# One batch's load in two transfers, weight blocks split beside two chunks, and some stages and closing sums at other places in the order

## The chip, the cores and the metric

The kernel runs on one core of one Trainium2 chip. The metric is the device time of one execution in microseconds, as the median of several executions. The engines of the core are named as in the profile: PE is TensorE (matmul; PEld its weight loads), DVE is VectorE, ACT is ScalarE, POOL is GpSimd, SP is SyncE, whose queue (SPq) issues most DMAs.

## The reference

```python
batch, seq, dim = (8, 3008, 256)          # x, float32
n_tokens, d_model, d_ff = (24064, 256, 2048)

X = np.fft.fft(x, axis=1)
X = np.fft.fft(X, axis=2)
attn = X.real.astype(np.float32)          # then reshaped to (24064, 256)

h = x @ w_in
relu6 = np.clip(h + 3.0, 0.0, 6.0)
g = h * relu6 / 6.0
return (g @ w_out).astype(np.float32)
```

So: a real part of a two-dimensional Fourier transform of each batch (over 3008 rows and 256 columns), and on its rows a two-layer MLP with a hardswish between the layers, all in float32.

## The kernel before

**Work and tiles.** The eight batches are taken as four pairs. The transform over 3008 = 47 x 64 rows has two stages. Stage 1 (`stage1`, eight blocks `c` per pair) works on four of the 64 columns at a time: SP loads x forward (`load_forward`, two transfers for the two batches of the pair, into partitions 0 to 63 and 64 on), POOL gathers the mirrored rows (`load_partners`), POOL adds and subtracts the two (`fold`, tiles `xt` and `y`), PE multiplies by a 47-row table, ACT and DVE copy the two PSUM banks to `z`, and SP sends `z` to a scratch in DRAM (`zd`). Stage 2 (`stage2`) loads it back turned round (`load_g`) and multiplies by 64-row tables; `split_q` writes its result as three parts into `KQ` (ACT the high part, DVE in `split_rest` the two others). The transform over the 256 columns is folded into `w_in`.

A pair has 12 chunks of about 256 rows (the chunk's number over all pairs is `n_all`, 0 to 47), a chunk eight steps `fc`, one for each 256 of the 2048 hidden columns. The first layer runs in units: PE adds the three passes of `KQ` times `KW` into the bank `u` (first the even half, then the odd one), ACT has put a first value into it (`seed`, u<-QN), a copy `s` of the even half is kept (`keep_even`), DVE forms the other sign `v` from `s` and `u` (`other_sign`), ACT takes the two ReLUs `t`, and DVE writes the gated hidden values into `A` (`gates`). The second layer multiplies 2 x 2 blocks with seven products (`mlp2`), of which POOL forms the sums `c` (`combine`). From chunk 8 on the first two of the seven products are not taken as float32 matmuls but as three passes each of a split operand `J` (`split_gates`: ACT twice, DVE twice) with split weights `GH` and `GK` (`split_weights`, once for each `fc`: ACT and DVE on 128 x 256 values, with a scratch bank `high`). At a chunk's end the seven sums are joined (`close`, parts 0 to 4: e<-acc, freeing the accumulator banks `acc` for the next chunk), POOL adds (`finish`), DVE transposes and SP sends the result (`store`).

**Order.** Every engine's order is written out by hand. From step `SPLIT` on the main loop runs in cycles, one unit each, with seven products of the second layer spread over it (six in the chunks before number 8); a cycle takes the pieces of the surrounding stages at fixed places: `products(1)`, `other_sign`, `close_to`, `passes`, `gates`, `products(size - 4)`, then the matmuls of stage 1 (`next(gen)`), `products(2)`, `split_rest`, `seed` of the unit after next, and the rest of stage 1. When the blocks of a pair are loaded and folded is decided by `Feed` and `fold_pieces`, which hold a planned backlog of POOL below a limit; `beside` puts stage 2 of chunk n at the step `when[n]`, counted from the unit that first uses it. The folding of pair p+1 lies in the chunks of pair p, on POOL between the sums `c`.

Of the kernel before, what the change touches and what calls it, by code (L numbers as in the profile page):

```python
# [60 lines left out]
def kernel(  # L61
# [121 lines left out]
    def load_forward(pr, c):  # L183
        xt = x_tile(xpool, "xf", 1)
        n = XC if c < NXC - 1 else XC - 1
        for b in range(2):

            i = 2 * pr.p + b
            nr = N1 + 1 if i < B - 1 else N1

            if b == 0:
                nr = PB
            rows, o = x_pn[i * N1:i * N1 + nr], xt[b * PB:b * PB + nr]
            nc.sync.dma_start(out=o[:, 0:n, :], in_=rows[:, c * XC + 1:c * XC + 1 + n, :])
            if n < XC:
                nc.sync.dma_start(out=o[:, n:XC, :], in_=rows[:, 0:1, :])
        pr.x[c] = xt
# [112 lines left out]
    def stage1(pr, c):  # L310
        y = pr.y[c]
        ps = [bank([P, 2, D], "ps1"), other_bank([P, 2, D], "ps1")]
        for h in range(2):
            last = (c, h) == (NXC - 1, 1)
            for b in range(2):
                n = 1 if last else 2
                nc.tensor.matmul(ps[b][h * PB:(h + 1) * PB, 0:n], table(0, b), y[rows(b), 2 * h:2 * h + n],  # L317
                                 start=True, stop=not last, skip_group_check=last)


            cosine, sine = slice(0, P + 1), slice(P + 1, D)
            for k, (j, cs) in enumerate([(XC - 1, cosine), (XC, cosine), (XC - 1, sine), (XC, sine)] if last else ()):
                for b in range(2):
                    nc.tensor.matmul(ps[b][h * PB:(h + 1) * PB, 1, cs], table(k + 1, b), y[rows(b), j, cs],
                                     start=False, stop=(k % 2 == 1), skip_group_check=True)
        z = zpool.tile([PB + PZ, 2, 2, D], F32, tag="z", name="z")
        nc.scalar.copy(z[:, 1], ps[1][0:PB + PZ])
# [233 lines left out]
    class Chunk:  # L561
# [3 lines left out]
        def __init__(self, pr, ck):  # L565
# [8 lines left out]
            self.n_all = pr.p * NCK + ck  # L574
            self.split, self.gated = self.n_all >= CHUNK2, {}
            k1 = [(ck * KK + j // 2 + 1) % NK1 for j in range(KC)]
# [234 lines left out]
    HIGH, OTHERS = (0,), (2, 1)  # L811

    def order_of(ch, fc):

        end = ch.final and fc == NF - 1
        if not ch.split:
            return [[(i, None)] for i in range(7)]
# [56 lines left out]
    def split_weights(fc):  # L874
# [9 lines left out]
        yield  # L884
        nc.scalar.mul(rest, ps[:], 1.0 / (1.0 + EPS))

    closing, freed = [], []

    def close_to(end):
        while closing and closing[0][1] < end:  # L890
            close(*closing[0])
            closing[0][1] += 1
            if closing[0][1] == 5:
                closing.pop()

    def close(ch, part):
# [12 lines left out]
        elif part == 3:  # L909
            plus(e[:, 5], 5, e[:, 0], -1.0)  # L910
        else:
            plus(e[:, 4], 4, e[:, 5])
            plus(e[:, 6], 6, e[:, 5])
            ch.r = {(m, h): ch.e[:, (1, 6, 2, 3)[2 * m + h]] for m in range(2) for h in range(2)}
# [332 lines left out]
    def beside():  # L1247
# [26 lines left out]
        for n in range(NSG, NP * NCK):  # L1274
# [9 lines left out]
            if i == 0:  # L1284
                put(max(t - 7, before + 1), load_t, gr)
                put(max(t - (6 if gr else 5), before + 1), load_g, pr, gr)
            put(t, stage2, pr, gr, i, at=middle_fns)
# [196 lines left out]
    for un in units:  # L1484
        for ch, _ in un.parts:
            first_use.setdefault(ch.n_all, place[max(un.i - 1, 0)] // 7)
    when = {n: first_use[n] - 7 for n in first_use}
    when[NSG - 1], when[NSG], when[NSG + 1] = 17, 23, 27
    prev = None
# [26 lines left out]
    for s in range(SPLIT):  # L1516
# [11 lines left out]
        else:  # L1528
# [7 lines left out]
            if prev and not prev.first:  # L1536
                turns_out(s)
            elif prev and 3 <= fc < 7:
                store(prev, (fc - 3) // 2, 1 - fc % 2)
            mlp2(*chunk(s), 0, 3)  # L1540
# [5 lines left out]
            mlp2(*chunk(s), 3, 7)  # L1546
            close_to(5)
        if fc == NF - 1:
# [5 lines left out]

    gates_of = {s: split_gates(*chunk(s)) for s in range(CHUNK2 * NF, len(steps))}
    high_of, others_of, others_at, start = [], [], 0, 0
    seed(units[1])
    weights_of = list(range(NF))

# [22 lines left out]
    def products(n):  # L1582
        nonlocal done, others_at
        for s, i in stream[done:done + n]:
# [4 lines left out]
            if fc == 0 and i == 6:  # L1589
                close_to(5)  # L1590
            flush(high_of, s)
# [4 lines left out]
            if i == 0:  # L1596
                high_of.extend(after.get(s, ()))
            if i in last or not last and i == 6:
                others_of.extend(after.get(s, ()))
# [4 lines left out]
    while done < len(stream):  # L1604
# [15 lines left out]
        flush(high_of)  # L1620
        if un:
            other_sign(un)
        close_to(5)
        if others_at > 4:
# [33 lines left out]
        split_rest()  # L1658
        if cycle + 2 < len(units):
            seed(units[cycle + 2])  # L1660
# [116 lines left out]
```

## Time and profile before

| | |
|---|---|
| median of three runs | 1820.53 us (1820.37 to 1821.40) |
| the profiled execution | 1819.84 us |
| its span, first to last instruction | 1818.1 us |
| mean granted TensorE clock | 0.997 |
| busy: PE, PEld, DVE, ACT, POOL | 98%, 84%, 81%, 76%, 72% |

Some 1.7 us of the profiled execution lie around the span. Idle time of PE is what can be saved; idle time of another engine counts only where PE waits for it. In the profile a row of the waits names who waited, for whom, the total, how often, and the longest; a row of the timeline has the start, the length, the engine, the line and the tiles, and in brackets the idle time before it and what ended it. Line numbers are those of the kernel before.

### The profile page before, as it was taken

The page shows a single profiled execution, that of the slowest core. Times are in us where ns is not written, and L with a number is a line of the kernel's source. Part 1 is how long each engine was busy: PE and PEld are TensorE (multiplying, and loading weights), DVE is VectorE, ACT ScalarE, POOL GpSimd, SP SyncE. Part 2 cuts the span into 40 slices and gives each one's busy share as a digit, 9 for nine tenths or more (in the row PEclk, how much of TensorE's full clock was granted, in tenths as well). Part 3 has the DMA queues.
Part 4 walks back from the last instruction along what each step waited for, and adds up shares of the span by engine and source line. Part 5 has one row for each costly group of instructions (what it writes and reads, how often), then busy time and mean ns, then how long its engine had stood idle before and what let it go on. Part 6 is the DMA issues. An engine that isn't in the chain of part 4 may idle for free.

```text
span 1818.1 us, 29912 instructions
## 1 busy us (share of the span) xinstructions
PE 1783.8 (98%) x9664; PEld 1524.8 (84%) x9664; DVE 1472.0 (81%) x2789; ACT 1382.1 (76%) x2496; POOL 1305.3 (72%) x1468
## 2 busy tenths in 40 slices
PE   9999999999999999999999999999999999999997
PEld 6678888868898888888898777888889888888897
DVE  8978555688888888888888777878888888888887
ACT  6556666678888788788888777778888888888884
POOL 5686787777678889766767877876766666676674
PEclk9999999999999999999999999999999999999999
DMA  8433341321213233111012232311101101101001
GB/s 276 117 95 80 94 107 46 75 58 47 47 38 90 68 80 86 46 44 44 15 48 79 65 76 56 81 43 47 38 21 48 36 21 44 42 18 45 20 14 32
DMA packets 160538, 110.36 MB, mean 61 GB/s; under 512 B 122292, under 2 KB 141074, under 8 KB 160382
## 3 DMA queue, kind: packets, MB, share of 16 engines
q1 hardware_dynamic: 151630, 82.22, 18.0%
q0 software_dynamic: 7504, 25.65, 4.6%
q8 instruction: 76, 1.25, 0.3%
q10 hardware_dynamic: 1248, 0.59, 0.1%
q14 instruction: 80, 0.66, 0.1%
HBM read 71.93 MB, written 36.79 MB: 60 GB/s over the span
## 4 chain that ended last, share of the span: by engine, by line
PE 85%; DVE 5%; DMA 3%; ACT 2%; POOL 2%; issue 1%; SPq 1%; ACTq 0%; DVEq 0%; POOLq 0%
PE acc L841 52%; PE u L702 24%; DMA xt<-in_x_dram 2%; PE ps L551 2%; PE ps L317 2%; PE acc L802 1%; POOL c L792 1%; PE v L601 1%; ACT t L775 1%; PE u L601 1%; DVE v L735 1%; SPq L963 1%; PE spare L1081 0%; DVE J L868 0%; DVE J L869 0%
## 5 line engine op out<-in xcount | busy, mean ns | idle before, releaser
L841 PE MATMUL acc<-c,G 128*128 128x256 f32 (+1 forms) x3008 | 766.5, 377 | 15.3 <-POOL c L792 11.3
L702 PE MATMUL u<-KQ,KW 128*128 128x512 f32 (+6 forms) x2448 | 744.7, 419 | 2.6 <-ACT s L725 2.6
L792 POOL TENSOR_TENSOR c<-A 128x512 f32<-128x512 f32 (+1 forms) x357 | 451.2, 1264 | 329.7 <-PE acc L841 309.5
L841 PEld LDWEIGHTS acc<-c,G 128*128 128x128 f32 x3008 | 535.4, 190 | 101.4 <-POOL c L792 22.2
L702 PEld LDWEIGHTS u<-KQ,KW 128*128 128x128 f32 (+1 forms) x2448 | 432.5, 189 | 67.1 <-ACT s L725 5.0
L775 ACT ACTIVATE t<-u,half 128x512 f32<-128x512 f32 (+2 forms) x384 | 260.8, 679 | 198.7 <-PE u L702 135.1
L735 DVE SCALAR_TENSOR_TENSOR v<-s,u 128x512 f32<-128x512 f32 (+1 forms) x360 | 246.9, 686 | 176.3 <-ACT t L775 172.4
L775 ACT ACTIVATE t<-v,half 128x512 f32<-128x512 f32 (+2 forms) x384 | 261.6, 681 | 134.0 <-DVE v L735 133.1
L778 DVE SCALAR_TENSOR_TENSOR A<-t,v 128x512 f32<-128x512 f32 (+3 forms) x478 | 250.1, 544 | 40.4 <-ACT t L775 38.5
L792 POOL TENSOR_TENSOR c<-c,A 128x256 f32<-128x256 f32 (+1 forms) x357 | 258.6, 724 | 28.0
L792 POOL TENSOR_TENSOR c<-A,c 128x256 f32<-128x256 f32 (+1 forms) x357 | 258.0, 723 | 28.0
L868 DVE SCALAR_TENSOR_TENSOR J<-high,A 128x512 fp32r<-128x512 f32 (+1 forms) x315 | 212.3, 674 | 67.5 <-ACT high L867 39.8
L841 PE MATMUL acc<-J,GK 128*128 128x256 f32 (+1 forms) x1260 | 257.7, 327 | 1.9 <-DVE J L869 1.7
L778 DVE SCALAR_TENSOR_TENSOR A<-t,u 128x512 f32<-128x512 f32 (+3 forms) x478 | 248.2, 540 | 0.0
L717 ACT ACTIVATE u<-QN,WN 128x512 f32<-128x512 f32 (+1 forms) x312 | 216.8, 695 | 0.3
L841 PE MATMUL acc<-A,G 128*128 128x256 f32 (+1 forms) x720 | 211.7, 375 | 0.5 <-DVE e L901 0.5
L869 DVE SCALAR_TENSOR_TENSOR J<-high,A 128x512 fp32r<-128x512 f32 (+1 forms) x315 | 210.7, 669 | 0.0
L841 PEld LDWEIGHTS acc<-J,GK 128*128 128x128 f32 x1260 | 193.6, 190 | 18.8 <-DVE J L869 3.8
L862 ACT ACTIVATE J<-A 128x512 fp32r<-128x512 f32 (+1 forms) x315 | 193.2, 613 | 0.0
L867 ACT COPY high<-J 128x512 f32<-128x512 f32 (+1 forms) x315 | 186.0, 590 | 8.8 <-DVE KQ L869 5.7
L725 ACT COPY s<-u 128x512 f32<-128x512 f32 (+2 forms) x315 | 179.2, 569 | 0.0
L841 PEld LDWEIGHTS acc<-J,GH 128*128 128x128 f32 x630 | 117.2, 189 | 25.0
(176 smaller groups left out, 1750.0 us busy)
## 6 DMA issues: line engine op xcount, KB each, us to landing
out_dram<-o SPq DMA_DIRECT2D x744, 32.0 KB
T<-in_c_stage_dram SPq DMA_DIRECT2D x26, 512.0 KB
g<-zd SPq DMA_DIRECT2D x42, 256.0 KB
zd<-z SPq DMA_DIRECT2D x48, 192.0 KB
QN<-qd SPq DMA_DIRECT2D x43, 128.0 KB
xt<-in_x_dram SPq DMA_DIRECT2D x21, 256.0 KB
st<-in_moe_w_out_dram POOLq DMA_DIRECT2D x7, 512.0 KB, 6.2
xt<-in_x_dram SPq DMA_DIRECT2D x17, 192.0 KB
```

The lines of the kernel that those rows point to most:

```text
L702: nc.tensor.matmul(un.wide(un.u[:]) if un.joint else un.u[:, i, 0:un.nq], un.weights(j, blk, i, rows), un.moving(j, blk, rows), start=Fals ...
L717: nc.scalar.activation(un.wide(un.u[:]), un.wide(row), AF.Identity, scale=WN[:, f:f + 1])
L725: copy(un.wide(un.s[:]), un.wide(un.u[:]))
L735: nc.vector.scalar_tensor_tensor(v, s, -2.0, u, op0=AL.mult, op1=AL.add)
L775: nc.scalar.activation(t, h, AF.Relu, bias=half[:], scale=scale)
L778: nc.vector.scalar_tensor_tensor(dst, t, 1.0, h, op0=AL.min, op1=AL.mult)
L792: (eng or nc.gpsimd).tensor_tensor(out, in0, in1, op=AL.add)
L841: nc.tensor.matmul(o, w, moving[i] if j is None else parts_tile(ch, fc)[:, j, i, 0:ch.n], start=(fc == 0 and i % 2 == 0 and j in (None, 0) ...
L862: nc.scalar.mul(high, a, 1.0 - EPS / 2.0)
L867: nc.scalar.copy(ps, high.bitcast(F32))
L868: nc.vector.scalar_tensor_tensor(low, ps, -1.0, a, op0=AL.mult, op1=AL.add)
L869: nc.vector.scalar_tensor_tensor(rest, ps, 1.0 + EPS, a, op0=AL.mult, op1=AL.subtract)
```

## The change

Seven edits, all in the order of things or in the engine that does them:

- **Load.** Where a batch's transfer has not more than 47 rows (only the last batch of the last pair: the others have 48 or 64), it is cut into one of 32 rows and one of 15.
- **Which products are split.** An even `fc` takes the split form from chunk 8 on as before, an odd one from chunk 9 on; the weights of the even ones are split beside chunk 7, those of the odd ones beside chunk 8, and none in a cycle in which a chunk ends.
- **Last step of a weight's split** (`rest`): DVE in place of ACT.
- **Closing sums.** The last part of `close` is cut in two: the sum of product 4 comes ahead of `other_sign`, that of product 6 behind it.
- **First chunk of a later pair.** Its stage 2 comes one step earlier (the load for it stays where it was).
- **Stage 1.** Its matmuls stand one product later where the step before had a stage 2; its copies come one further point later, behind the seed of the unit after next.
- **Store of the first chunk**: the transposes of its second half one step later.

```diff
 # load_forward
-            nc.sync.dma_start(out=o[:, 0:n, :], in_=rows[:, c * XC + 1:c * XC + 1 + n, :])
-            if n < XC:
-                nc.sync.dma_start(out=o[:, n:XC, :], in_=rows[:, 0:1, :])
+            cut = nr if nr > N1 else N1 // 16 * 16
+            for r in (slice(0, cut), slice(cut, nr))[:1 + (cut < nr)]:
+                nc.sync.dma_start(out=o[r, 0:n, :], in_=rows[r, c * XC + 1:c * XC + 1 + n, :])
+                if n < XC:
+                    nc.sync.dma_start(out=o[r, n:XC, :], in_=rows[r, 0:1, :])
 # stage1, between the matmuls and the copies
+        yield
         z = zpool.tile([PB + PZ, 2, 2, D], F32, tag="z", name="z")
 # order_of, the planner and the main loop
+    def split_of(ch, fc):
+        return ch.n_all >= CHUNK2 + fc % 2
-        if not ch.split:
+        if not split_of(ch, fc):
...
-    weights_of = list(range(NF))
+    weights_of = [fc + (CHUNK2 - 1 + fc % 2) * NF for fc in (*range(0, NF, 2), *range(1, NF, 2))]
 # split_weights
-        nc.scalar.mul(rest, ps[:], 1.0 / (1.0 + EPS))
+        nc.vector.tensor_scalar(rest, ps[:], 1.0 / (1.0 + EPS), None, op0=AL.mult)
 # close
-        else:
-            plus(e[:, 4], 4, e[:, 5])
+        elif part == 4:
+            plus(e[:, 4], 4, e[:, 5])
+        else:
             plus(e[:, 6], 6, e[:, 5])
 # beside, and the steps of stage 2
-                put(max(t - (6 if gr else 5), before + 1), load_g, pr, gr)
+                put(max(t - (6 if gr else 4), before + 1), load_g, pr, gr)
+    for p in range(1, NP):
+        when[p * NCK] -= 1
 # the first chunk's store
-            elif prev and 3 <= fc < 7:
-                store(prev, (fc - 3) // 2, 1 - fc % 2)
+            elif prev and fc in (3, 4, 6, 7):
+                store(prev, fc // 5, (fc + 1) % 2 if fc < 5 else fc % 2)
 # the main loop's cycle
         if un:
+            close_to(5)
             other_sign(un)
-        close_to(5)
+        close_to(6)
...
-        if weights_of and not stages and done >= 7 * ((CHUNK2 - 1) * NF + weights_of[0] + 1 - SPLIT):
-            splitting = split_weights(weights_of.pop(0))
+        if weights_of and not stages and not ends and done >= 7 * (weights_of[0] + 1 - SPLIT):
+            splitting = split_weights(weights_of.pop(0) % NF)
...
-        products(size - 4)
+        behind_it = 1 if any(s - 1 in middle_fns for s in begun) else 2
+        products(size - 2 - behind_it)
         for gen in parts:
             next(gen)
-        products(2)
+        products(behind_it)
+        if parts and cycle + 2 < len(units):
+            seed(units[cycle + 2])
+        for gen in parts:
+            next(gen)
```

**Place 1, SP's queue** in the chunks of the third pair (where the last batch is loaded): `xt<-in_x_dram` are the forward loads, `out_dram<-o` the stores, `g<-zd` and `g<-zq` the loads of stage 2, `zd<-z` the sends of stage 1. Before:

```order
L963 DMA out_dram<-o 4x32x64 x6
L194 DMA xt<-in_x_dram 64x1024
L194 DMA xt<-in_x_dram 47x1024
L468 DMA g<-zd 64x4x256
L471 DMA g<-zq 64x4x1
L468 DMA g<-zd 64x4x256
```

and with the change:

```order
L971 DMA out_dram<-o 4x32x64 x6
L196 DMA xt<-in_x_dram 64x1024
L196 DMA xt<-in_x_dram 32x1024
L196 DMA xt<-in_x_dram 15x1024
L471 DMA g<-zd 64x4x256
L474 DMA g<-zq 64x4x1
L471 DMA g<-zd 64x4x256
```

The 47-row transfer has become one of 32 and one of 15 rows; the loads of stage 2 behind it stand one issue later, and nothing else in the queue has moved.

**Place 2, DVE** at the start of the second pair's first chunk: `J` are the two DVE steps of a product's split, `KQ` those of stage 2's result, `e<-acc` the closing sums of the chunk before. Before:

```order
L901 SCALAR_TENSOR_TENSOR e<-acc,e 128x256 x2
L868 SCALAR_TENSOR_TENSOR J<-high,A 128x512
L869 SCALAR_TENSOR_TENSOR J<-high,A 128x512
L639 SCALAR_TENSOR_TENSOR KQ<-ps_4376,KQ 128x2x256
L640 SCALAR_TENSOR_TENSOR KQ<-KQ,ps_4376 128x2x256
L735 SCALAR_TENSOR_TENSOR v<-s,u 128x450
L901 SCALAR_TENSOR_TENSOR e<-acc,e 128x256 x2
L778 SCALAR_TENSOR_TENSOR A<-t,u 128x256
```

and with the change:

```order
L908 SCALAR_TENSOR_TENSOR e<-acc,e 128x256 x2
L875 SCALAR_TENSOR_TENSOR J<-high,A 128x512
L876 SCALAR_TENSOR_TENSOR J<-high,A 128x512
L908 SCALAR_TENSOR_TENSOR e<-acc,e 128x256
L738 SCALAR_TENSOR_TENSOR v<-s,u 128x450
L908 SCALAR_TENSOR_TENSOR e<-acc,e 128x256
L781 SCALAR_TENSOR_TENSOR A<-t,u 128x256
```

The two KQ steps have left for the cycle before, and the two last closing sums stand on the two sides of `v`; at the other chunk ends only the second of these moves is found.

**Place 3, ACT** in chunk 7, where weights are split: `GK<-GH` and `GK<-high` are the first and last step of a weight's split, `u<-QN` the seed, `t` the ReLUs. Before:

```order
L725 COPY s<-u 128x512
L878 ACTIVATE GK<-GH 128x256
L717 ACTIVATE u<-QN,WN 128x512
L885 ACTIVATE GK<-high 128x256
L775 ACTIVATE t<-u,half 128x512
```

and with the change:

```order
L728 COPY s<-u 128x512
L885 ACTIVATE GK<-GH 128x256
L720 ACTIVATE u<-QN,WN 128x512
L778 ACTIVATE t<-u,half 128x512
L778 ACTIVATE t<-v,half 128x512
```

The last step of the split is gone from between the seed and the ReLU on ACT; on DVE it now stands behind the four steps that it depends on.

More of the change, by code (lines that the diff above doesn't have):

```diff
@@ L574, in __init__ @@
             self.n_all = pr.p * NCK + ck
-            self.split, self.gated = self.n_all >= CHUNK2, {}
+            self.gated = {}
             k1 = [(ck * KK + j // 2 + 1) % NK1 for j in range(KC)]
@@ L892, in close_to @@
             closing[0][1] += 1
-            if closing[0][1] == 5:
+            if closing[0][1] == 6:
                 closing.pop()
@@ L1553 @@
     done = 0
-    gates_of = {s: split_gates(*chunk(s)) for s in range(CHUNK2 * NF, len(steps))}
+    gates_of = {s: split_gates(*chunk(s)) for s in range(CHUNK2 * NF, len(steps)) if split_of(*chunk(s))}
     high_of, others_of, others_at, start = [], [], 0, 0
     seed(units[1])
-    weights_of = list(range(NF))
+    weights_of = [fc + (CHUNK2 - 1 + fc % 2) * NF for fc in (*range(0, NF, 2), *range(1, NF, 2))]
     def turn_before(s):
@@ L1589, in products @@
             if fc == 0 and i == 6:
-                close_to(5)
+                close_to(6)
             flush(high_of, s)
@@ L1597, in products @@
                 high_of.extend(after.get(s, ()))
-            if i in last or not last and i == 6:
+            if i in last or not last and i == 3:
                 others_of.extend(after.get(s, ()))
@@ L1621 @@
         if un:
+            close_to(5)
             other_sign(un)
-        close_to(5)
+        close_to(6)
         if others_at > 4:
@@ L1658 @@
         split_rest()
-        if cycle + 2 < len(units):
+        if not parts and cycle + 2 < len(units):
             seed(units[cycle + 2])
```

## The prediction

> **What bounds the kernel now.** I read the page's busy times first, then whom PE waited for, then equal stretches of the run against each other.
>
> ```profile
> PE 1783.8 (98%) x9664; PEld 1524.8 (84%) x9664; DVE 1472.0 (81%) x2789; ACT 1382.1 (76%) x2496; POOL 1305.3 (72%) x1468
> PE acc L841 <- POOL c L792: 11.3, 6, 3.8
> PE acc L841 <- DVE e L901: 3.3, 5, 0.9
> PE u L702 <- ACT s L725: 2.6, 5, 0.9
> PE v L601 <- DVE a L778: 2.5, 3, 2.0
> PE acc L841 <- DVE J L869: 1.7, 4, 0.7
> ```
>
> PE is busy for 1783.8 of 1818.1 us, so an order of things can win at most 34 us; the named waits hold 21 us of them, and half of that is one wait for POOL's sums c. The next view, busy time by stretch, says where. The stretches run from the start of chunk 12 to that of chunk 24 (pair 1), and from there to that of chunk 36 (pair 2): the same matmuls, 2327 in both.
>
> ```profile
> 461.20:893.30 432.10, 430.84 (x2327) 372.29 (x2325) 362.63 (x681) 351.66 (x634) 329.46 (x365) 1.00 0.23 58
> 893.30:1341.60 448.30, 435.63 (x2327) 373.79 (x2325) 363.42 (x681) 351.90 (x634) 328.62 (x365) 0.99 0.22 56
> ```
>
> Pair 2 takes 448.30 - 432.10 = 16.2 us more for equal work. What differs is the batch it loads beside: the last one, whose transfer has 47 rows where pair 1's has 48. In the waits from 993 to 1205 us, in those from 560 to 773 us, and in the chain of waits, the load is seen (rows in this order):
>
> ```profile
> POOL xt L271 <- DMA xt<-in_x_dram: 40.0, 7, 9.4
> POOL xt L271 <- DMA xt<-in_x_dram: 7.4, 4, 2.3
> 993.00 11.43 DMA xt<-in_x_dram
> ```
>
> POOL stands 40.0 us for x against 7.4 us, and one 47-row transfer takes 11.43 us. The timeline shows the same block of both pairs: SP issues the two loads, POOL then folds.
>
> ```profile
> 560.24 1.16 SPq L194 DMA_DIRECT2D xt<-in_x_dram  x2
> 565.10 1.27 POOL L271 TENSOR_TENSOR xt<-xt 111x508 f32<-111x508 f32 x1 [1.33 <-DMA xt<-in_x_dram]
> 992.41 1.02 SPq L194 DMA_DIRECT2D xt<-in_x_dram  x2
> 1004.59 1.26 POOL L271 TENSOR_TENSOR xt<-xt 111x508 f32<-111x508 f32 x1 [8.66 <-DMA xt<-in_x_dram]
> ```
>
> Pair 1 folds 565.10 - 560.24 = 4.9 us after the first issue, pair 2 only 12.2 us after it. During the landing, the stretches show (the last two columns are the share of the 16 DMA engines and GB/s)
>
> ```profile
> 561.60:563.80 2.20, 2.20 (x14) 1.94 (x14) 2.20 (x6) 1.96 (x4) 2.02 (x3) 1.00 0.87 224
> 999.60:1003.40 3.80, 3.80 (x22) 2.33 (x21) 1.74 (x4) 2.18 (x5) 0.00 (x0) 1.00 0.10 26
> 1007.70:1011.10 3.40, 2.92 (x9) 2.57 (x10) 0.76 (x2) 0.09 (x1) 3.24 (x5) 0.50 0.00 0
> 1130.60:1134.00 3.40, 3.40 (x10) 2.94 (x11) 1.26 (x2) 0.00 (x0) 3.32 (x5) 0.51 0.00 0
> ```
>
> 224 GB/s over nearly all engines in pair 1, and 26 GB/s over a tenth of them in pair 2, about what one or two engines of sixteen give. The sums c queue on POOL behind the fold, PE runs dry for up to 3.8 us, and after that its granted clock is 0.50 for 3.4 us, which costs another 1.7 us; the last row is the second such place.
>
> **The change part by part** (a minus is a gain).
>
> *The load, -16.0.* In the changed queue the last piece is issued one DMA later (half of 1.16 us, 0.6). If its 15 rows go the slow way, they take 15/47 of 11.43 = 3.6 us at most; if they spread as the 48 rows do, they land as in pair 1. So the fold comes between 4.9 + 0.6 = 5.5 and about 6.5 us after the first issue, not 12.2. PE's longest wait here was 3.8 us, so a fold up to 12.2 - 3.8 = 8.4 us after the issue stops nothing. Both ends clear it by 1.9 us or more, so I take all of the 16.2 but 0.2 for the extra issues on SP, which has idle time. Bounds: 14 to 16.2. Late next is nothing that pair 1 doesn't show, with 1.3 us of waiting at the fold and none of it on PE.
>
> The page "DMA: Bandwidth & Descriptors" of the Trainium skill (Why a DMA increments its semaphore by 16 and not by 1) says that a transfer runs on the largest number of engines up to 16 that divides its outermost size: 1 for 47, 16 for 48 and 32, 15 for 15. The 0.10 against 0.87 agrees; by it the 15 rows land early, and the sum would be 0.2 lower.
>
> *First chunk of pairs 1 to 3, -2.6.* DVE and PE there:
>
> ```profile
> 892.84 0.68 DVE L640 SCALAR_TENSOR_TENSOR KQ<-KQ,ps 128x512 fp32r<-128x512 f32 x1
> 893.43 0.62 DVE L735 SCALAR_TENSOR_TENSOR v<-s,u 128x450 f32<-128x450 f32 x1
> 893.97 0.75 DVE L901 SCALAR_TENSOR_TENSOR e<-acc,e 128x256 f32<-128x256 f32 x2
> 894.44 1.56 PE L841 MATMUL acc<-c,G 128*128 128x256 f32 x6 [0.86 <-DVE e L901]
> ```
>
> The closing sum frees the bank that PE wants 0.86 us earlier. With both KQ steps gone and one sum ahead of v, it is 2 x 0.6 + 0.5 = 1.7 us earlier, and the wait goes, at three places. The KQ steps fall into the cycle before, where DVE copies s early and v has a whole cycle of room. Bounds: -2.6 to -1.
>
> *A closing sum ahead of v, +1.2.* Everywhere else it pushes v, and behind it t<-v and s on ACT, by half of 0.75, which PE's next passes wait for. Two chunk ends show the room:
>
> ```profile
> 824.18 0.58 ACT L725 COPY s<-u 128x512 f32<-128x512 f32 x1
> 825.32 1.06 PE L702 MATMUL u<-KQ,KW 127*128 127x512 f32 x3
> 496.70 0.58 ACT L725 COPY s<-u 128x512 f32<-128x512 f32 x1
> 497.41 0.77 PE L702 MATMUL u<-KQ,KW 127*128 127x512 f32 x2
> ```
>
> The first has 825.32 - 824.76 = 0.56 us, enough for 0.37. The second, behind a pair's last chunk, has 0.13 and loses 0.25; that is found three times (0.75), and I add 0.45 for ends between the two. Bounds: 0.5 to 4.
>
> *Weights beside two chunks, -1.8.* The waits of PE from 340 to 420 us, where the weights are split and the split products begin:
>
> ```profile
> PE u L702 <- ACT s L725: 1.4, 2, 0.9
> PE acc L841 <- DVE J L869: 1.3, 3, 0.7
> PE acc L841 <- DVE e L901: 0.7, 2, 0.5
> 352.96 0.38 ACT L885 ACTIVATE GK<-high 128x256 fp32r<-128x256 f32 x1 [1.38 <-DVE high L883]
> ```
>
> Together 3.4 us. ACT's ReLU stands behind a step that waits 1.38 us for DVE; on DVE that step costs its own 0.4 us ahead of v instead. With a split in every other cycle and none at a chunk's end, I let 2.4 of the 3.4 go; the rest stays, since one cycle still has four or five weight steps, two J steps, v and the gates on DVE. Against it stand four odd fc of chunk 8 with float32 products. The chain of waits prices them (4 matmuls: 2 split and 2 float32; 12: 4 and 8):
>
> ```profile
> 557.19 0.67 PE acc L841 x4
> 558.56 2.20 PE acc L841 x12
> ```
>
> From 2s + 2f = 0.67 and 4s + 8f = 2.20, f = 0.215 and s = 0.12 us. Two products cost 4f = 0.86 in float32 and 6s = 0.72 split, so +0.14 for each fc, +0.6 in all. Bounds: -2.8 to +1.
>
> *Stage 1 and the store, 0.* ACT waits 1.47 us for stage 1's matmuls, and the seed (0.69) now stands in that gap:
>
> ```profile
> 594.14 0.59 ACT L327 COPY z<-ps 112x512 f32<-112x512 f32 x1 [1.47 <-PE ps L317]
> 595.40 0.69 ACT L717 ACTIVATE u<-QN,WN 128x512 f32<-128x512 f32 x1
> ```
>
> Without that cover, 0.69 us on ACT in 24 cycles. The 2.0 us for `a` at v L601 lie behind a weight step that stays. Bounds: -0.5 to +3.
>
> Sum: -16.0 - 2.6 + 1.2 - 1.8 = -19.2. From the profiled execution's 1819.84 us (span 1818.1) this gives 1800.6; the median of the runs lies 0.7 above it, so 1801.3.
>
> **The rivals.**
>
> *Slower: the time is one for each odd transfer, not for its rows* (0.05). Then the 15-row piece also takes 11.4 us, begins 0.6 us later, and decides as soon as it lands after what the 47 rows did. Eight folds later by 0.6 to 1.1 us (7 us, since PE is already dry there), and two more waits long enough to halve the clock (2 x 1.7), make +10.4; less 3.2 for the other edits, 1828. Against it: 26 GB/s in the landing says that bytes go through few engines.
>
> *The transfers are no faster cut in two* (0.07). All of the 16.2 stays, and the other edits give 1820.5 - 3.2 = 1817.3. The same page of the Trainium skill (Rules for kernel authors) says not to bother with two transfers to disjoint partitions, as both spray over the same 16 engines and serialize. This rule speaks against the change. For it in the trace: the pieces have one queue. Against it: the 47 rows are not spread at all, with 0.10 of the engines busy.
>
> *New waits take part of it* (0.07): the closing sum and the stage-1 copies both at their upper bounds, +2.8 and +3, the weights at +1 (2.8 worse) and the load at -14 (2 worse) give 1811.9.
>
> **How the numbers follow.** The main case has 0.81. Its lower end is every term at its good end: -16.2 - 2.6 + 0.5 - 2.8 - 0.5 = -21.6, 1798.9, less 2.4 if the waits for `a` and the last of the weights' go as well: 1796.5. Its upper end is 1809: load at -14 and two of the other terms bad. That holds 8 in 10. The measurement can tell 0.2%, 3.6 us, from no change: the main case and the third rival lie below 1816.9 (0.88), the second rival within (0.07), the first above (0.05).
>
> **What would show it.** Pair 2's twelve chunks at 432 to 434 us instead of 448.3; POOL's wait for x from 993 to 1205 us near 8 instead of 40 us; a granted clock of 1.00 all through; no wait for e at the starts of chunks 12, 24 and 36; under 1.5 us of PE's waits from 340 to 420. The prediction is wrong if the 15-row transfer lands later than 8 us after the first issue, or if PE waits for s or J at chunk ends or in stage-1 cycles by over 4 us in all.

## The result, and the profile after

| | before | after |
|---|---|---|
| median of the runs | 1820.76 us (1820.37 to 1821.40, 4 runs) | 1791.70 us (1791.60 to 1792.14, 4 runs) |
| the profiled execution, its span | 1819.84 us, 1818.1 us | 1791.71 us, 1789.9 us |
| mean granted TensorE clock | 0.997 | 0.999 |

The ratio is 0.9841, with a 95% interval of 0.9823 to 0.9858. The change gains 29.1 us, where 19.2 were forecast: the direction and the largest term are right, and the time lies 4.8 us below the lower end of the range.

The page's busy times after, then of e_load (the load edit alone, see below), and four rows of PE's waits in the whole run after (those left out lie in the first 26 us or come to 0.2 us):

```profile
PE 1773.1 (99%) x9656; PEld 1519.5 (85%) x9656; DVE 1468.3 (82%) x2789; ACT 1374.6 (77%) x2480; POOL 1306.4 (73%) x1468
PE 1778.8 (99%) x9664; PEld 1523.9 (85%) x9664; DVE 1470.5 (82%) x2789; ACT 1381.5 (77%) x2496; POOL 1306.5 (72%) x1468
PE acc L848 <- DVE c L795: 2.0, 2, 1.0
PE u L705 <- ACT s L728: 1.2, 3, 0.4
PE acc L848 <- DVE J L876: 0.6, 2, 0.4
PE v L604 <- DVE a L781: 0.5, 2, 0.3
```

PE's 11.3 us of waiting for POOL's c have gone, and so has all waiting for e. But PE's busy time fell too, from 1783.8 to 1773.1 us, with 8 matmuls fewer of 9664. So the 1783.8 were not all work. The load edit alone takes 5.0 of these 10.7 us, nearly all in the third pair, whose mean granted clock was 0.99 before and is 1.00 with the load cut. The other edits take 5.7 us, and this is in the main waiting that the view counts as work. Here, and at named waits that it left standing, the forecast went short.

The same two stretches of 2327 matmuls as in the prediction, found in the changed kernel by the same matmuls (busy time by stretch):

```profile
453.95:883.89 429.94, 429.51 (x2327) 370.75 (x2325) 362.02 (x681) 351.34 (x634) 329.29 (x365) 1.00 0.23 58
883.89:1313.93 430.04, 429.62 (x2327) 370.79 (x2326) 362.15 (x681) 351.35 (x634) 329.44 (x365) 1.00 0.23 58
```

Both take 430 us now: the second lost 18.3 us, of which the first lost 2.2 as well. (The prediction names these stretches after chunks 12, 24 and 36. They begin at the marks where stage 2 of the next pair's first chunk is split, which is two chunks earlier, in chunks 10, 22 and 34. The comparison is of equal work all the same. Place 2 shows such a mark too, and not the second pair's first chunk itself.)

The load in the changed kernel, first as POOL's waits for x from 983 to 1193 us, then as the timeline of the block that the prediction showed:

```profile
POOL xt L273 <- DMA xt<-in_x_dram: 7.9, 4, 2.4
```
```profile
982.13 1.63 SPq L196 DMA_DIRECT2D xt<-in_x_dram  x3
986.98 1.27 POOL L273 TENSOR_TENSOR xt<-xt 111x508 f32<-111x508 f32 x1 [1.32 <-DMA xt<-in_x_dram]
```

POOL waits 7.9 us instead of 40.0, and the fold begins 986.98 - 982.13 = 4.85 us after the first issue instead of 12.2.

**Where the time went.** To place the rest, I set the starts of the same `u` passes of PE (its passes of `KQ` times `KW`, counted from the first) against each other in the traces. This measures from start to start, so a wait counts whether the view calls it idle or busy. Columns: start in us of pass 0, then the length of five stretches up to passes 360, 540, 1320, 1620 and 2400. The later rows are those of the experiments below.

```
              pass 0    to 360   to 540   to 1320   to 1620   to 2400
before         165.0     155.4    139.2     525.8     250.3     536.5
after          163.6     155.0    133.8     522.7     232.8     535.6
e_load         166.2     155.4    139.2     525.7     234.1     536.4
e_weights      166.5     155.4    134.2     525.7     251.6     536.4
e_rest         166.9     155.4    137.7     525.8     251.6     536.4
e_stage1       166.2     155.0    138.4     524.8     250.8     536.8
e_s1later      168.2     155.0    138.6     525.8     250.2     536.5
e_s1copies     165.8     155.4    139.0     525.1     251.0     536.8
e_close        168.5     155.4    139.7     523.6     251.5     535.7
e_store        164.4     155.4    139.2     525.7     251.8     536.5
e_noload       164.7     155.0    133.8     522.8     249.2     535.6
e_cut43        165.4     155.0    133.8     522.7     250.6     535.7
e_cut46        164.6     155.0    133.8     522.9     238.1     535.6
```

The weights are split in the second stretch (320 to 460 us), the last batch is loaded in the fourth (985 to 1236 us). After against before: -1.4, -0.4, -5.4, -3.1, -17.5 and -0.9, which is -28.6 us by pass 2400. Behind it the changed kernel takes 0.5 us longer (46.4 us to the end of the span, where before takes 45.9). Not every difference in this table belongs to an edit: in before and the single edits that leave the load as it was, the fourth stretch varies from 250.2 to 251.8 us, mostly at one place between passes 1416 and 1440, and pass 0 varies too (see the store).

### The profile page after: what moved, and what is told of

It reads as the page before. It is cut to its first block, busy times and chain, and to the rows that moved or that the text cites. A ratio compares the mean times of both kernels' runs of the same rounds, so it can differ in the third digit from the quotient of the medians.

```text
span 1789.9 us, 29894 instructions
## 1 busy us (share of the span) xinstructions
PE 1773.1 (99%) x9656; PEld 1519.5 (85%) x9656; DVE 1468.3 (82%) x2789; ACT 1374.6 (77%) x2480; POOL 1306.4 (73%) x1468
## 4 chain that ended last, share of the span: by engine, by line
PE 93%; DVE 4%; ACT 2%; issue 1%; DMA 0%; ACTq 0%; DVEq 0%; SPq 0%
PE acc L848 57%; PE u L705 27%; PE ps L554 2%; PE ps L319 2%; PE acc L805 1%; PE v L604 1%; PE u L604 1%; ACT t L778 1%; DVE v L738 1%; PE spare L1089 0%; PE ps L517 0%; DVE J L876 0%; DVE xt L236 0%; DVE J L875 0%; ACT s L728 0%
## 5 line engine op out<-in xcount | busy, mean ns | idle before, releaser
L875 DVE SCALAR_TENSOR_TENSOR J<-high,A 128x512 fp32r<-128x512 f32 (+1 forms) x311 | 209.6, 674 | 65.5 <-ACT high L874 46.4
L848 PE MATMUL acc<-J,GK 128*128 128x256 f32 (+1 forms) x1244 | 253.1, 325 | 0.6 <-DVE J L876 0.6
L876 DVE SCALAR_TENSOR_TENSOR J<-high,A 128x512 fp32r<-128x512 f32 (+1 forms) x311 | 207.6, 667 | 0.0
L848 PEld LDWEIGHTS acc<-J,GK 128*128 128x128 f32 x1244 | 190.0, 189 | 16.8 <-DVE J L876 2.1
```

What stands on the lines that cost most here:

```text
L848: nc.tensor.matmul(o, w, moving[i] if j is None else parts_tile(ch, fc)[:, j, i, 0:ch.n], start=(fc == 0 and i % 2 == 0 and j in (None, 0) ...
L875: nc.vector.scalar_tensor_tensor(low, ps, -1.0, a, op0=AL.mult, op1=AL.add)
L876: nc.vector.scalar_tensor_tensor(rest, ps, 1.0 + EPS, a, op0=AL.mult, op1=AL.subtract)
```

## The experiments

The kernel before ran beside each group: medians 1822.5, 1822.0 and 1822.9 us in the three groups. Its single runs spread from 1819.8 to 1825.4 us (68 runs); the changed kernel has four runs, within 0.5 us. More on that under the store and in the last section.

**The load alone (e_load).** The first hunk of the diff, and nothing else:

```diff
+            cut = nr if nr > N1 else N1 // 16 * 16
+            for r in (slice(0, cut), slice(cut, nr))[:1 + (cut < nr)]:
```

> The kernel before with the load edit alone (32 and 15 rows for the last batch). The two traces put 16.2 us of the gain into the third pair, where the load is. Theory A (the load edit alone makes that gain): -16 us, about 1804.7 us, the third pair's stretch at 432 to 433 us instead of 448.3 and everything ahead of 880 us as before. Rival (the third pair also gains from the other edits, with the load as less than all of it): -12 us or less. Rival (the odd transfer costs by itself): no gain.

Measured: 1806.0 us, 16.5 below the kernel before beside it, ratio 0.9911 (0.9897 to 0.9924). The same two stretches in its trace:

```profile
462.24:894.31 432.07, 430.81 (x2327) 372.27 (x2326) 362.38 (x681) 351.64 (x634) 329.62 (x365) 1.00 0.23 58
894.31:1326.45 432.14, 430.88 (x2327) 372.25 (x2326) 362.60 (x681) 351.65 (x634) 329.64 (x365) 1.00 0.23 58
```

The third pair now takes what the second takes, to 0.1 us, and every other stretch of the table is as before (pass 0 begins 1.2 us later). The load edit holds 250.3 - 234.1 = 16.2 us by itself, and up to 17.7 us against the longest of the other fourth stretches, e_store's.

**All but the load (e_noload).** The changed kernel with the first hunk undone:

```diff
-            for r in (slice(0, cut), slice(cut, nr))[:1 + (cut < nr)]:
+            nc.sync.dma_start(out=o[:, 0:n, :], in_=rows[:, c * XC + 1:c * XC + 1 + n, :])
```

> The changed kernel with the last batch's transfer left whole (47 rows): all edits but the load. Theory (the edits add up, the load alone holds the third pair's 16 us): 1808 us, 16 us over the changed kernel, the third pair's stretch longer by 14 to 18 us with waits of POOL for x and places of half clock, and 12.5 us under the kernel before. Rival (the other edits give the third pair slack that hides part of the slow transfer): under 1803 us. Rival (without the load cut the other edits give nothing that lasts): over 1814 us.

Measured: 1809.6 us, ratio 0.993 (0.9915 to 0.9946). The fourth stretch is 249.2 - 232.8 = 16.4 us longer than in the changed kernel, and all others are equal to it, but for a start 1.1 us later. The load edit and the others add up; none hides part of another.

**Two other cuts of the same 47 rows (e_cut43, e_cut46).** The changed kernel with the cut at 43 and 4 rows, and at 46 and 1:

```diff
-            cut = nr if nr > N1 else N1 // 16 * 16
+            cut = nr if nr > N1 else 43    # e_cut46: 46
```

> The changed kernel with the last batch's transfer cut into 43 and 4 rows instead of 32 and 15: two transfers as well, and as many DMAs. Theory (it is the 47 as a number, the rows that one transfer spreads over the engines, not that there are two): 43 rows go as slowly as the 47, 43/47 of 11.4 us is 10.5 us, the fold comes about 11 us after the first issue, PE runs dry by about 1 us less at each of eight folds, and 6 to 13 us of the 16 come back: 1798 to 1805 us. By the Trainium skill's page DMA: Bandwidth & Descriptors (Why a DMA increments its semaphore by 16 and not by 1) 43 goes on one engine and 4 on four, which is the same forecast. Rival (two transfers in place of one is what helps, whatever their sizes): as the changed kernel, 1792 us, fold 5 to 6 us after the first issue. Rival (the time is one for each odd transfer, not for its rows): all 16 us come back.

> The changed kernel with the cut at 46 and 1 rows. The 43 rows went at 26 GB/s like the 47, and their fold came 12.05 us after the first issue (47 rows: 12.27; 32 and 15: 4.85). Theory (a transfer goes over as many engines as divide its rows, so 46 over two): 46 rows of 4 KB at 52 GB/s take 3.6 us where 47 at 26 GB/s take 7.4, so the fold comes 8.8 us after the first issue, near the 8.4 up to which nothing stops: 1792 to 1796 us, a stretch of two tenths of the engines at about 52 GB/s. Rival (all row counts that are not multiples of 16, or above 16, go over one engine): fold at 12 us, 1808 to 1810 us. Rival (only 47 and 43, as primes, are slow, other counts go over all engines): fold at 5 to 5.5 us, 1792 us.

Measured: 1809.8 us for 43 and 4 (ratio 0.9928, 0.9913 to 0.9943), 1798.2 us for 46 and 1 (0.9868, 0.9853 to 0.9883). The folds of the block, 43 rows first, then 46:

```profile
983.88 1.37 SPq L196 DMA_DIRECT2D xt<-in_x_dram  x3
995.93 1.27 POOL L273 TENSOR_TENSOR xt<-xt 111x508 f32<-111x508 f32 x1 [8.54 <-DMA xt<-in_x_dram]
```
```profile
983.29 1.35 SPq L196 DMA_DIRECT2D xt<-in_x_dram  x3
992.24 1.26 POOL L273 TENSOR_TENSOR xt<-xt 111x508 f32<-111x508 f32 x1 [5.41 <-DMA xt<-in_x_dram]
```

And what moved while POOL stood, by stretch (last two columns: share of the 16 DMA engines, GB/s), again 43 first:

```profile
990.00:994.00 4.00, 4.00 (x23) 2.50 (x22) 2.54 (x4) 2.88 (x6) 0.00 (x0) 1.00 0.08 25
```
```profile
989.50:992.00 2.50, 2.50 (x16) 1.81 (x17) 1.97 (x3) 2.25 (x5) 0.00 (x0) 1.00 0.14 45
```

43 rows run at 25 GB/s over 0.08 of the engines, as the 47 do at 26 over 0.10, and the fold comes 12.05 us after the first issue. 46 rows run at 45 GB/s over 0.14, not quite twice that, and the fold comes after 8.95 us (8.8 expected). So it isn't that there are two transfers: with 43 and 4 rows all of the 16 us are lost again. Nor is every odd count slow, since the 15 rows of the change land with the 32. The Trainium skill, page "DMA: Bandwidth & Descriptors" (Why a DMA increments its semaphore by 16 and not by 1), has the rule that fits all five sizes: the largest number up to 16 that divides the rows, 1 for 47 and 43, 2 for 46, 15 and 16 for 15 and 32. Both times missed their expectation. For 43 the 11.4 us had been scaled by the rows, but some 4.9 us of a fold's delay are there with a fast transfer too. If only the rest goes with the rows, the fold comes after 11.6 us; why it came at 12.05 stays open. For 46 the fold was right, but what it costs was not: 0.55 us past the limit of 8.4 us would be 4.4 us over eight folds, and the fourth stretch is 238.1 - 232.8 = 5.3 us longer; pass 0 begins another 1.0 us later.

**The weights (e_weights), and their last step alone (e_rest).** e_weights has all hunks on which products are split and where the weights are split; e_rest has one line of them, shown below. They include an edit that the list of seven doesn't name: in a step without split products the second part of the next split is due behind the fourth product instead of the seventh.

```diff
-        nc.scalar.mul(rest, ps[:], 1.0 / (1.0 + EPS))
+        nc.vector.tensor_scalar(rest, ps[:], 1.0 / (1.0 + EPS), None, op0=AL.mult)
```

> The kernel before with the weights edits alone (even weights beside chunk 7, odd ones beside chunk 8, none at a chunk's end, the last step on DVE, and four odd fc of chunk 8 with float32 products). The prediction's term: -1.8 us (2.4 us of named waits less 0.6 for the float32 products). Theory from the two traces (spacing of equal matmuls from 345 to 420 us, in which stretched busy time counts as well): -5.4 us, all of it between 340 and 425 us. Rival (the cycles gain but chunk 8 gives it back): within 1 us of the kernel before.

> The kernel before with only the last step of a weight's split on DVE in place of ACT (the order of splits and of products as before). The weights edits together gave -6.7 us from 345 to 415 us and +1.7 behind it. Theory (ACT's ReLU stood behind a step that waited 1.4 us for DVE, eight times in all): -2 to -5 us from 345 to 420 us, most of what the edits together gain. Rival (the gain is that of spreading the splits over two chunks, since DVE, not ACT, was full in these cycles): within 0.8 us or a loss, as DVE has 0.4 us more in each of eight cycles. The prediction's term cannot tell the two apart.

Measured: 1817.7 us for all of them (ratio 0.9975, 0.9966 to 0.9985), 1821.6 us for the line alone (0.9997, 0.9988 to 1.0006). In the table the second stretch falls by 139.2 - 134.2 = 5.0 us with all, by 1.5 us with the line alone. So moving the step off ACT is by itself the smaller part. The same stretch of passes (438 to 480) in the kernel before and in e_weights, as busy time by stretch (PE, PEld, DVE, ACT, POOL):

```profile
377.30:414.80 37.50, 35.21 (x169) 26.68 (x168) 32.41 (x61) 28.43 (x56) 29.13 (x35) 1.00 0.22 58
```
```profile
376.20:409.70 33.50, 33.28 (x164) 27.13 (x162) 28.09 (x54) 23.80 (x44) 29.16 (x35) 1.00 0.25 64
```

DVE has 54 instructions in it instead of 61 (4.3 us less), ACT 44 instead of 56 (4.6 us less), and the stretch is 4.0 us shorter. Which of the two queues the rest hangs on isn't separated. PE's busy time falls by 1.9 us, though only five matmuls differ. Where that busy waiting sits is seen in PE's timeline of before:

```profile
381.02 0.40 PE L841 MATMUL acc<-J,GH 128*128 128x256 f32 x2
381.96 0.70 PE L841 MATMUL acc<-A,G 128*128 128x256 f32 x2 [0.55 <-DVE e L901]
...
383.20 0.59 PE L841 MATMUL acc<-c,G 128*128 128x256 f32 x2
384.44 0.74 PE L841 MATMUL acc<-J,GK 128*128 128x256 f32 x4 [0.65 <-DVE J L869]
```

In an undisturbed cycle of the same kernel the next matmul begins 0.24 us behind two such J matmuls (422.88 to 423.12 us) and 0.25 us behind two c matmuls (424.24 to 424.49). So here it could have begun at 381.26; it began at 381.96, 0.70 us late, where the row names 0.55. Behind the c matmuls it is 383.45 against 384.44, 0.99 late, named 0.65. A matmul's modelled end lies behind the point at which the next could follow. The weight loads' own waits from 340 to 420 us in the kernel before (without those of stage 1 and those of issue) come nearer:

```profile
PEld acc L841 <- DVE J L869: 3.1, 4, 1.1
PEld u L702 <- ACT s L725: 2.9, 4, 1.3
PEld acc L841 <- DVE e L901: 1.1, 2, 0.8
PEld u L702 <- ACT u L717: 0.5, 2, 0.3
```

7.6 us here, against 3.4 us on PE's rows. By the starts of the passes, e_weights gains 7.1 us up to pass 474 and gives 2.0 us back up to pass 504, where its last two splits and the last float32 products of chunk 8 lie; that leaves the 5.0 of the table. How the gain is shared between fewer splits in a cycle, none at a chunk's end, the earlier second part, and chunk 8's four unsplit fc wasn't tried.

**Stage 1 (e_stage1), and its two halves (e_s1later, e_s1copies).** All three hunks together, then only the matmuls one product later, then only the copies behind the seed:

```diff
 # e_s1later
-        products(size - 4)
+        behind_it = 1 if any(s - 1 in middle_fns for s in begun) else 2
+        products(size - 2 - behind_it)
...
-        products(2)
+        products(behind_it)
 # e_s1copies
+        if parts and cycle + 2 < len(units):
+            seed(units[cycle + 2])
+        for gen in parts:
+            next(gen)
```

> The kernel before with the stage-1 edits alone (matmuls one product later behind a step with a stage 2, copies one point later behind the seed). The prediction's term: 0 (-0.5 to +3). Theory from the two traces: -3 us, as 0.1 to 0.7 us in each of about 24 cycles, with no named wait of PE that goes: the wait is one of the weight loads for the gates' products (14 waits with 9.1 us before, 12 with 4.2 in the changed kernel), which lies under matmuls that count as busy. Rival (the gain belongs to other edits that share these cycles): within 0.5 us.

> The kernel before with only one half of the stage-1 edits: its matmuls one product later behind a step with a stage 2 (the copies where they were). Both halves gave about -3 us in the trace, where the weight loads of stage 1 waited 4.8 instead of 9.1 us for DVE's gated values A. Theory (the stage-1 matmuls stood in PE's queue ahead of the gates that free their bank, and one product more covers that): -2.5 to -3 us by itself, with waits of stage 1's weight loads for A at 4 to 5 us. Rival (the seed in ACT's gap ahead of the copies gives it): within 0.7 us.

> The other half: the copies of stage 1 one point later, behind the seed (the matmuls where they were). Theory (the matmuls' place gives the -3 us): within 0.7 us, waits of stage 1's weight loads for A near 9 us as before. Rival (the seed in ACT's gap of 1.5 us gives it): -2.5 to -3 us. The prediction held that 0.69 us on ACT in 24 cycles is covered here and worth nothing to PE.

Measured: 1819.1 us together (ratio 0.9979, 0.9970 to 0.9988), 1821.9 (0.9996, 0.9987 to 1.0006) and 1821.5 us (0.9998, 0.9989 to 1.0007) for the halves. Up to pass 1320 the table gives -2.2 us together and -1.0 and -0.9 for the halves (the three stretches up to there, each against before). Both theories of one half fell: each half does its part, by another mechanism. The groups of stage 1's instructions (busy, mean ns | idle before, by whom), in before, e_s1later and e_s1copies:

```profile
L317 PE MATMUL ps<-y,F 47*64 47x512 f32 x192 | 40.3, 601 | 0.4 <-DVE A L778 0.3
L327 ACT COPY z<-ps 112x512 f32<-112x512 f32 x24 | 14.0, 585 | 36.5 <-PE ps L317 29.3 <-PE ps L324 5.7 <-issue 1.5
L317 PEld LDWEIGHTS ps<-y,F 47*64 47x64 f32 x192 | 9.3, 131 | 18.2 <-DVE A L778 9.1 <-issue 8.0
```
```profile
L317 PE MATMUL ps<-y,F 47*64 47x512 f32 x192 | 36.2, 601 | 0.1
L327 ACT COPY z<-ps 112x512 f32<-112x512 f32 x24 | 14.1, 586 | 36.8 <-PE ps L317 29.6 <-PE ps L324 5.7 <-issue 1.5
L317 PEld LDWEIGHTS ps<-y,F 47*64 47x64 f32 x192 | 9.1, 131 | 14.0 <-issue 8.0 <-DVE A L778 4.8
```
```profile
L317 PE MATMUL ps<-y,F 47*64 47x512 f32 x192 | 40.3, 601 | 0.4 <-DVE A L779 0.3
L328 ACT COPY z<-ps 112x512 f32<-112x512 f32 x24 | 14.0, 585 | 22.0 <-PE ps L317 18.1 <-PE ps L324 3.9
```

The later matmuls halve the weight loads' wait for DVE's gated values, 9.1 to 4.8 us, and 4.1 us of "busy" matmul time go with it, for which PE had 0.4 us of idle to show. The copies behind the seed leave that wait as it was, and take ACT's standing for stage 1 from 36.5 to 22.0 us. Of each, only about 1 us reaches the starts of PE's passes up to pass 1320, and the medians of the halves can't be told from no change.

**Closing sums and the first chunk (e_close).** The hunks on `close`, `close_to`, `load_g` and `when` alone:

```diff
+    for p in range(1, NP):
+        when[p * NCK] -= 1
...
+            close_to(5)
             other_sign(un)
-        close_to(5)
+        close_to(6)
```

> The kernel before with the two edits on closing sums and on the first chunk of a later pair (stage 2 a step earlier, a closing sum ahead of v). The prediction's terms: -2.6 at three starts of chunks, +1.2 at the other chunk ends, -1.4 in all. Theory from the two traces: -2.3 at the three starts (461, 893 and 1342 us) and 0 at the other ends, -2.3 in all. Rival (the closing sum ahead of v is paid at every chunk's end, hidden in the changed kernel by other edits): +0 or more, with new waits of PE for s or v.

Measured: 1821.4 us, ratio 0.9991 (0.9982 to 1.0000). The median says little, since this kernel's runs lie between 1817.8 and 1825.2 us. By the table it is +0.5 up to pass 540, -2.2 up to 1320 and -0.8 in the last stretch, -2.5 us together. Pass 540 lies inside the first of the three starts, so the +0.5 is no price of its own: pass by pass, the chunk ends ahead of this start cost 0.1 us, the three starts gain 0.4, 0.8 and 0.7 us, and from the first start to the second another 0.5 us goes. The price for the sum ahead of v appears behind pass 2400: there e_close takes 0.5 us more, as the changed kernel does, and in both PE waits twice for DVE's c in the last chunk, where the kernel before has one such wait.

**The store (e_store).** One hunk:

```diff
-            elif prev and 3 <= fc < 7:
-                store(prev, (fc - 3) // 2, 1 - fc % 2)
+            elif prev and fc in (3, 4, 6, 7):
+                store(prev, fc // 5, (fc + 1) % 2 if fc < 5 else fc % 2)
```

> The kernel before with the store edit alone (the transposes of the first chunk's second half one step later). The prediction's term: 0; it put the 2.0 us wait of PE for the gated values at v (131 us) down to a weight step that stays. Theory from the two traces: the wait is that of DVE's transpose for the send of the chunk's first half, so -1.9 us at 131 us, and no half clock at 132 to 138 us, which the e_close run shows there (0.70 and 0.87) and the first profile of before does not: -2 us against a run without it, -3.5 us against a run with it, all ahead of 165 us. Rival (prediction): within 0.5 us ahead of 165 us, and the same wait of PE for the gated values.

Measured: 1819.8 us, ratio 0.9986 (0.9977 to 0.9995). In the kernel before, the waits from 120 to 142 us and DVE's timeline:

```profile
PE v L601 <- DVE a L778: 2.0, 1, 2.0
DVE o L958 <- DMA out_dram<-o: 1.9, 1, 1.9
```
```profile
126.45 0.45 DVE L958 STREAM_TRANSPOSE o<-e 128x256 f32<-128x256 f32 x1 [1.88 <-DMA out_dram<-o]
126.82 0.83 DVE L610 SCALAR_TENSOR_TENSOR s<-QN,WN,u 128x256 f32<-128x256 f32 x2
```

The transpose for the send waits 1.88 us for the buffer that a DMA is still reading, at the head of DVE's queue, and s, u, v and the gates stand behind it. In e_store neither of the two waits is left at this place.

The start itself varies: pass 0 begins between 165.0 and 168.5 us in the profiles of the eight kernels with the old store (166.7 in the mean), and between 163.6 and 165.4 us in those of the six with the new one (164.5). Against the first profile of before e_store therefore shows only -0.6 us, against the mean of the eight -2.3, where -1.9 was worked out; the medians of the runs differ by 2.2. A look at the granted clock (third from the right) shows one reason. First before, then e_close, then e_store, at the same place:

```profile
132.00:136.00 4.00, 4.00 (x22) 2.58 (x21) 3.25 (x6) 2.40 (x5) 2.43 (x3) 1.00 0.18 41
```
```profile
132.00:136.00 4.00, 3.12 (x9) 2.58 (x10) 3.83 (x8) 1.16 (x2) 2.55 (x5) 0.70 0.07 16
```
```profile
130.00:134.00 4.00, 4.00 (x23) 2.53 (x22) 3.60 (x8) 1.44 (x3) 3.92 (x5) 1.00 0.00 0
```

The same wait of 2.0 us costs the clock behind it in one execution and not in another. All eight profiles with the old store have it. In the 4 us behind it the granted clock is 0.65 in e_s1later and 0.59 in e_close, whose pass 0 begins at 168.2 and 168.5 us, and 1.00 in the six others, which begin it by 166.9. What spreads those six over 1.9 us stays open.

**One step more (e_tail).** The changed kernel's own rows show PE waiting twice for a sum c on DVE in the last chunk. There DVE and POOL begin a sum in the same moment (1767.88 and 1767.85 us), and DVE's takes 1.38 us; alone it takes 0.54 (columns of the timeline as above):

```profile
1767.88 1.38 DVE L795 TENSOR_TENSOR c<-A 128x384 f32<-128x384 f32 x1
1777.30 0.54 DVE L795 TENSOR_TENSOR c<-A 128x384 f32<-128x384 f32 x1
1767.85 0.99 POOL L795 TENSOR_TENSOR c<-A 128x384 f32<-128x384 f32 x1 [0.20 <-PE acc L848]
```

```diff
-        eng = nc.vector if ch.final and fc % 2 and fc > 2 else nc.gpsimd
+        eng = nc.vector if ch.final and fc in (4, 7) else nc.gpsimd
```

> The changed kernel with one step more: in the last chunk the sums c of fc 4 and 7 are on DVE, the others on POOL (in the changed kernel those of 3, 5 and 7 are on DVE). The changed kernel's trace shows PE waiting twice 1.0 us for DVE's c at 1769 and 1775 us, where that sum takes 1.38 us on DVE beside a sum of POOL's that starts at the same time, and 0.54 us alone. Theory: the second wait goes and the first is halved: -1.5 us, 1790.2 us. Rival (POOL's queue, with 2.1 us of other sums ahead of fc 3, is as late): within 0.5 us of 1791.7 us, with PE waiting for POOL's c there.

Measured: 1789.82 us (1789.54 to 1790.01, 5 runs), ratio to the kernel before 0.9822 (0.9809 to 0.9836). It lies below all of the changed kernel's runs, by 1.9 us in the medians, though the two did not run beside each other; from pass 2400 to the end its trace takes 2.2 us less than the changed kernel's (44.2 against 46.4), which is where the edit lies. Neither wait of PE for c is left in its trace, so the first one went whole and not by half as expected: POOL's sum for fc 3 began at 1766.80 us, one of its two other sums behind it. This is the fastest version here.

## Why the prediction was right in direction and short in size

| term | forecast | by the starts of the same passes |
|---|---|---|
| load | -16.0 | -16.2 (e_load) |
| closing sums, first chunk | -2.6 + 1.2 | -2.5 (e_close: +0.5, -2.2, -0.8), and +0.5 behind pass 2400 |
| weights beside two chunks | -1.8 | -5.0 (e_weights) |
| stage 1 | 0 | -0.4 - 0.8 - 1.0 = -2.2 up to pass 1320 (e_stage1), -1.3 in the fourth stretch (after against e_load) |
| store, the start | 0 | -1.4 (pass 0, after against before) |
| sum, up to pass 2400 | -19.2 | -28.6 |

The -1.3 of stage 1 in the fourth stretch comes in four steps of 0.3 us (near passes 1372, 1420, 1516 and 1564), and e_stage1 steps down at the same passes. The medians of the five single edits lie 16.5, 4.8, 3.5, 1.2 and 2.2 us below the kernel before that ran beside each (load, weights, stage 1, closing sums, store), 28.2 us in all.

- **Load: right.** The block, the row (a 47-row transfer over a tenth of the engines) and the fold at 4.85 us, where 5.5 to 6.5 was worked out, all came as forecast. POOL's wait for x is 7.9 us (near 8 forecast), and the clock is 1.00 through the third pair. The rivals "no faster cut in two" and "a time for each odd transfer" are both refuted by e_load. The Trainium skill's rule not to bother with two transfers (page "DMA: Bandwidth & Descriptors", Rules for kernel authors) gives as its reason that both halves spread over all 16 engines. The 47 rows did not (0.10 of the engines), and the cut gained 16.2 us, so the rule doesn't hold here; whether it holds for transfers that are already spread, no run shows.
- **The premise failed.** "An order of things can win at most 34 us; the named waits hold 21 of them" took busy PE for working PE. The order edits gained 12.4 us (28.6 less 16.2), while their forecast was 3.2. Between the profiles of e_load and of the changed kernel PE's busy time falls by 5.7 us and its idle time by 7.3. The 5.7 were out of the forecast's sight, since PE's rows show only the part of a wait that isn't covered by the modelled end of the matmul before. The rest of the shortfall lies in named waits that were to stay and went, the store's 2.0 us among them, and in a price of 1.2 us that did not come in the main loop.
- **Weights: mechanism half right, size wrong.** The step that failed is "together 3.4 us, I let 2.4 go". Up to pass 474 the edits gained 7.1 us; the weight loads' rows had 7.6. Behind it 2.0 us came back, where +0.6 was forecast for the float32 products, a price that stands untested by itself. The step on ACT that the prediction put first is worth 1.5 of the 5.0.
- **Stage 1: "zero" failed.** The prediction saw the seed in ACT's gap as cover and asked only what it might cost. The row that was not read is PEld's wait of 9.1 us, 14 times, for the gates, under matmuls that count as busy. By the starts of the passes both halves of the edit gain.
- **Store: "behind a weight step that stays" failed.** It named the wrong instruction on DVE. The transpose that waits for the DMA begins at 126.45 us on DVE, 0.37 us ahead of the first step of s, and what PE waits for stands behind it. With the store moved, the 2.0 us at v are gone.
- **Closing sums: right at the three starts** (0.7 to 0.8 each in the changed kernel against e_load, 0.4 to 0.8 in e_close; 0.86 forecast). The +1.2 for the other ends did not come: they cost 0.1 us ahead of the first start, and 0.5 us came in the last chunk alone. The chunk end at 496.70 us, where the prediction read 0.13 us of room and a loss, shows no wait of PE for s after. The three waits of 0.4 us for ACT's s in the rows stand about 60 us behind the three starts, before and after alike.
- **What would show it:** the twelve chunks of pair 2 take 430.0 us, below the 432 to 434 of the forecast, by the 2.1 us that pair 1 gained as well. The other signs came: no wait for e is left at the three starts, and from 338 to 417 us, which holds the work of 340 to 420 before, PE has no wait in the rows at all (under 1.5 us was forecast).

## What to carry to other kernels

Take what a reordering can win from the spacing of the same instructions, and from the weight loads' waits as an upper end (7.6 us for the 7.1 gained at the weights, 4.3 for 1.0 at stage 1's matmuls), not from the idle share of the matmul engine: a matmul that can't be followed looks busy. Where one batch is slower than its twin, look at the row count of its transfers before the queue: 47 rows kept a tenth of the DMA engines busy, and a cut into 32 and 15 gave back all 16.2 us where 43 and 4 gave back none. An instruction that waits for a DMA at the head of an engine's queue is found in that engine's own waits, and what stands behind it pays: 2.0 us of PE here.

## What the runs showed of the hardware that was not expected

A wait of PE of 2.0 us lowered the granted clock behind it, to 0.65 and 0.59 over 4 us, in two of eight executions at one and the same place, and left it at 1.00 in six. Between 120 and 1240 us the profile of before has two places with a granted clock below 0.95, e_noload one, e_stage1 and e_weights three, e_close four, and the changed kernel none. The kernel before spread over 5.6 us in 68 runs and over 1.0 in the four that ran beside the changed kernel, the changed one over 0.5 in four. That these places cause the spread fits, but was not tried by itself. A sum on DVE that starts together with one of the same shape on POOL took 1.38 us instead of 0.54, while POOL's took 0.99 to 1.01 either way.
